# Phase 3 of a convolution and spectral-mix kernel on two 64-row tiles of the array

## The chip, the cores and the metric

The kernel runs on one core of a Trainium2 chip. The metric is device time in microseconds of one execution, the median of several runs. The core has a tensor engine (TensorE, PE in the profile, its weight loads PEld), a vector engine (VectorE, DVE), a scalar engine (ScalarE, ACT), GpSimd (POOL), and SyncE (SP), which here issues the transfers to DRAM.

## The reference

The input x has 8 batches, 3264 positions and 192 channels. First comes a causal convolution over 7 positions whose weights are a softmax per head (8 heads of 24 channels). Its result, called x from here on, goes through a spectral mix:

```
X = np.fft.rfft(x, axis=1)                        # the first 64 modes are kept
Yr = einsum('bmd,mde->bme', Xr, w_r) - einsum('bmd,mde->bme', Xi, w_i)
Yi = einsum('bmd,mde->bme', Xr, w_i) + einsum('bmd,mde->bme', Xi, w_r)
y = np.fft.irfft(Y, n=S, axis=1)
u = x + y
return u + np.maximum(u @ w_ch, 0.0)
```

The output is float32, 8 x 3264 x 192.

## The kernel before

A batch's 3264 positions are cut into 27 windows of 122 positions; a window is held as 128 rows, of which the last 6 belong to the next window too. `x_all` holds all of it in bf16, positions on the partitions.

Phase 1 loads x (GpSimd issues the transfers, which also change the type), convolves on TensorE with banded matrices, and sums the Fourier transform of the 64 modes. Phase 2 mixes the modes, four at a time on four column tiles of the array (`mix`, L387 to L402), and beside each group of modes it transposes pieces of `x_all` on TensorE (`t_next`, L354 to L370). The transposes go to `cTs[p]`, one for each pair p of batches: for each window first 128 channels of one batch, then 128 channels of the other, and then, in a slot for both, the remaining 64 channels of the one in rows 0 to 63 and of the other in rows 64 to 127 (its source is copied together by `make_tail`, L317). In the version before, pair p holds batches b and b + 2 with b from `pair_batch`.

Phase 3 computes the output. A group is half the batches, h, and a window w: four batches, two banks of PSUM, one bank for k = 0 and one for k = 1, each with two batches of 192 columns. The steps of one group are

- `group_g(..., 0, ...)` (L455): for each bank one product of the inverse transform's matrix `gst` (64 modes, real and imaginary parts, so 128 rows) with `zw`, the mixed modes already multiplied by w_ch; 384 columns. This is y @ w_ch.
- `group_ab` (L436): x @ w_ch, for each batch a product over 128 channels (L446) and one over the remaining 64 (L452), 192 columns each. For the second, the stationary operand has 128 rows, 64 of each batch of the pair; the moving operand `wB0` or `win1` holds w_ch's last 64 rows against the batch's own and zeros against the others.
- `relu` (L460) on ScalarE, in place in PSUM, both banks at once.
- `finish_group` (L467): `group_g` with part 1 adds y itself to the bank (384 columns again), VectorE adds x and writes the tile `t` (L470), and SP sends `t` to DRAM (L484), one transfer for a group, or two where a window must not write over the next one's rows.

The order is written out by hand (`tc.manual_schedule()`); each engine works through its own queue in that order, and semaphores are put in where data pass between engines. `seq` (L486 to L491) runs nine steps over three chains of windows, 0 to 8, 9 to 17 and 18 to 26, alternating the two halves h. A window's transfer writes 128 rows; the last 6 are not its own and are overwritten by the next window of the same batches, so the next window's transfer waits until this one has landed. SP's queue is in order, so whatever stands behind waits as well.

Groups are finished two behind the one whose products start. The first two groups get their x @ w_ch part before the last group of modes is mixed (L501 to L503, with a zeroing product over 384 columns, L439, since their first product then isn't the spectral one). Their spectral part follows the first half of the `zw` products (L524 to L528), and their ends follow the second half. Four PSUM tiles of two banks each (pools `pza`, `pzb`) go round; `t` has eight buffers (pool `p3`).

Of the kernel before, what the change touches and what calls it, by code (L numbers as in the profile page):

```python
# [9 lines left out]
ALU = mybir.AluOpType  # L10
ACT = mybir.ActivationFunctionType
AX = mybir.AxisListType
F32 = mybir.dt.float32
BF16 = mybir.dt.bfloat16
PSUM = bass.MemoryType.PSUM
# [3 lines left out]
def kernel(  # L19
# [9 lines left out]
    nc = tc.nc  # L29
    B, S, D = x.shape  # L30
# [5 lines left out]
    P = 128  # L36
    WIN = 122
    OV = KK - 1
    NWIN = 27
# [14 lines left out]
    x_all = constp.tile([P, B, NWIN, D], BF16, tag="x_all")  # L54
# [30 lines left out]
    xt = ep.tile([P, 4, 2 * B, MODES], BF16, tag="xt")  # L85
# [39 lines left out]
    for b in range(2, B):  # L125
        for u in range(3):
# [8 lines left out]
                            in0=sidx[:, :].unsqueeze(2).to_broadcast([P, NWIN, MODES]),  # L135
                            in1=midx[:, :].unsqueeze(1).to_broadcast([P, NWIN, MODES]),
                            op=ALU.mult)
# [8 lines left out]
                            in1=wmax[:, :].unsqueeze(2).to_broadcast([P, H, KK]), op=ALU.subtract)  # L146
# [24 lines left out]
    for k in range(KK):  # L171
        nc.vector.copy_predicated(
            out=cband[:, 0:4, :],
            mask=maskk[:, k, :].bitcast(mybir.dt.uint16).unsqueeze(1).to_broadcast([P, 4, P]),
            data=wpv[:, 0:4, k:k + 1].to_broadcast([P, 4, P]))
        for j in range(4):
# [3 lines left out]
                         start=(k == 0), stop=(k == KK - 1))  # L180
# [17 lines left out]
    win0 = constp.tile([P, 2 * D], BF16, tag="win0")  # L198
    win1 = constp.tile([P, 2 * D], BF16, tag="win1")
    wB0 = constp.tile([P, D], BF16, tag="wB0")  # L200
# [11 lines left out]
    gst = constp.tile([P, GW], BF16, tag="gst")  # L212
# [93 lines left out]
    conv_stack.close()  # L306
    workp = early_stack.enter_context(tc.tile_pool(name="work", bufs=2, side="right"))
    tailp = early_stack.enter_context(tc.tile_pool(name="tails", bufs=3, side="right"))
    pza = ctx.enter_context(tc.tile_pool(name="pza", bufs=2, space=PSUM))
    ps2 = ExitStack()  # L310
    pt = ps2.enter_context(tc.tile_pool(name="pt", bufs=4, space=PSUM))

    def pair_batch(p):
        return 4 * (p // 2) + p % 2

    tails = {}

    def make_tail(p, w0, n):  # L320
        b = pair_batch(p)
        tl = tailp.tile([P, 7, 2, D - P], BF16, tag="tail", name="tail")
        nc.vector.tensor_copy(out=tl[0:WIN, 0:n, :, :],
                              in_=x_all[0:WIN, b:b + 3:2, w0:w0 + n, P:D].rearrange("p b w e -> p w b e"))
        for w in range(w0, w0 + n):
            tails[(p, w)] = tl[0:WIN, w - w0, :, :].rearrange("p b e -> p (b e)")

    def slot_lhsT(p, k):
        b = pair_batch(p)
        r, w = divmod(k, NWIN)  # L330
        if r < 2:
            return x_all[0:WIN, b + 2 * r, w, 0:P]
        return tails[(p, w)]

    cTs = {}

    chunks = []
    for p in range(4):
        k = 0
        for i in range(11):  # L340
            n = 8 if i < 4 else 7
# [49 lines left out]
    def mix(g):  # L391
        zt = pt.tile([P, 512], F32, tag="p", name="yp")
        for j in range(3):
            for pos in range(4):
                m = MG * g + pos
                nc.tensor.matmul(zt[32 * pos:32 * pos + 32, 0:D],  # L396
                                 xt[:, j:j + 2, :, m].rearrange("p j k -> p (j k)"), wtiles[g][:, pos, j, :],
                                 start=(j == 0), stop=(j == 2), tile_position=(0, 32 * pos))
        ymix = workp.tile([P, D], BF16, tag="ymix")
        nc.scalar.copy(out=ymix[:], in_=zt[:, 0:D])  # L400
        return zt, ymix
# [7 lines left out]

    zwi = {}
    wBs = (wB0[:, :], win1[:, 0:D])

    def zw_mm(o, h, part, k):
        for i in range(2):
            b = 4 * h + 2 * k + i
            for e, wn in ((0, win0), (1, win1)):
                nc.tensor.matmul(o[:, D * i:D * i + D],
                                 yeT[:, e, :, :].rearrange("p m (c b) -> p (m c) b", c=2)[:, :, b],  # L420
                                 wn[:, D * part:D * part + D], start=(e == 0), stop=(e == 1),
                                 skip_group_check=True)
# [10 lines left out]
                nc.scalar.activation(out=zt[:], in_=zp[:, 0:2 * D], func=ACT.Copy, scale=ascale[:, 0:1])  # L433
            zwi[(h, part, k)] = zt[:]

    def group_ab(h, w, zp, first):  # L436
        if first:
            for k in range(2):
                nc.tensor.matmul(zp[:, k, 0:2 * D], xt[:, 3, 0:2, :].rearrange("p a m -> p (a m)"),  # L439
                                 win0[:, :], start=True, stop=False,  # L440
                                 skip_group_check=True)
        for k in range(2):
            for i in range(2):
                p, r = 2 * h + i, k
                c0 = WIN * (NWIN * r + w)
                nc.tensor.matmul(zp[:, k, D * i:D * i + D], cTs[p][:, c0:c0 + P], win0[:, 0:D],  # L446
                                 start=False, stop=False, skip_group_check=True)
        for i in range(2):
            for k in range(2):
                p = 2 * h + i  # L450
                c0 = WIN * (2 * NWIN + w)
                nc.tensor.matmul(zp[:, k, D * i:D * i + D], cTs[p][:, c0:c0 + P], wBs[k],  # L452
                                 start=False, stop=(i == 1 and not first), skip_group_check=True)

    def group_g(h, w, zp, part, first, last):  # L455
        for k in range(2):
            nc.tensor.matmul(zp[:, k, 0:2 * D], gst[:, WIN * w:WIN * w + P], zwi[(h, part, k)],  # L457
                             start=first, stop=last, skip_group_check=True)

    def relu(zp):  # L460
        nc.scalar.activation(out=zp[:, :, 0:2 * D], in_=zp[:, :, 0:2 * D], func=ACT.Relu)  # L461

    CH = 9

    def finish_group(h, w, zp):  # L467
        group_g(h, w, zp, 1, False, True)
        t = p3.tile([P, B // 2, D], F32, tag="t", name="t")
        nc.vector.tensor_tensor(  # L470
            out=t[:].rearrange("p (k i) e -> p k i e", k=2),
            in0=zp[:, :, 0:2 * D].rearrange("p k (i e) -> p k i e", i=2),
            in1=x_all[:, 4 * h:4 * h + 4, w, :].rearrange("p (k i) e -> p k i e", k=2),
            op=ALU.add)
        if w == NWIN - 1:
            rows = ((0, 80), (80, LASTVALID))
        elif w % CH == CH - 1:
            rows = ((0, 112), (112, WIN))
        else:
            rows = ((0, P),)  # L480
        for r0, r1 in rows:
            dst = bass.AP(tensor=out.tensor, offset=out.offset + (4 * h * S + WIN * w + r0) * D,
                          ap=[[D, r1 - r0], [S * D, B // 2], [1, D]])
            nc.sync.dma_start(out=dst, in_=t[r0:r1, :, :])  # L484

    steps = [(0, 0), (0, 1)]  # L486
    for st in range(CH):
        steps.append((1, st))
        if st + 2 < CH:
            steps.append((0, st + 2))  # L490
    seq = [(h, st + CH * c) for h, st in steps for c in range(3)]  # L491

    ahead(0)
    gq = [0, 1]
    zps = []
    for g in range(NGRP):
        last = g == NGRP - 1
        if last:
            while tpos[0] < len(chunks):
                t_next(3)  # L500
            zps = [pza.tile([P, 2, 512], F32, tag="z", name="z") for _ in range(2)]  # L501
            for n in range(2):
                group_ab(*seq[n], zps[n], True)  # L503
        m = mix(g)
        if g == 6:
            wts0_stack.close()
            cTb = ctx.enter_context(tc.tile_pool(name="stashb", bufs=1)).tile([P, CTW], BF16, tag="cTb")
            nc.vector.memset(cTb[:, NSLOT * WIN:CTW], 0.0)
            cTs[3] = cTb[:, :]
        if g in (0, 1, 2):  # L510
            load_weights(g + 7, wp)
        elif 7 <= g and g + 3 < NGRP:
            load_weights(g + 3, wp)
        if not last:
            for _ in range(1 if g < 7 else 2):
                t_next(2 if g < 6 else 3)
            if gq and g % 2 == 1:
                g_part(gq.pop(0))
        mix_t(g, *m)
    early_stack.close()  # L520
    p3 = ctx.enter_context(tc.tile_pool(name="p3", bufs=8, side="right"))
# [1 line left out]

    zw_part(0, 0)  # L524
    zw_part(0, 1)
    for n in range(2):
        group_g(*seq[n], zps[n], 0, False, False)
        relu(zps[n])  # L528
    zw_part(1, 0)
    zw_part(1, 1)  # L530
    for n in range(2):
        finish_group(*seq[n], zps[n])
    ps2.close()
    pzb = ctx.enter_context(tc.tile_pool(name="pzb", bufs=2, space=PSUM))

    zq = []
    for n in range(2, len(seq)):
        h, w = seq[n]
        zp = (pzb, pza)[n // 2 % 2 == 0].tile([P, 2, 512], F32, tag="z", name="z")
        group_g(h, w, zp, 0, True, False)  # L540
        group_ab(h, w, zp, False)
        relu(zp)
        zq.append((h, w, zp))
        while len(zq) > (2 if n < len(seq) - 6 else 1):
            finish_group(*zq.pop(0))
    while zq:
        finish_group(*zq.pop(0))

# [1 line left out]
_INS = ['x', 'weight', 'moe_w_r', 'moe_w_i', 'moe_w_ch']  # L550
# [26 lines left out]
```

## Time and profile before

| what | us |
|---|---|
| median of 3 runs | 196.57 (196.34 to 198.24) |
| the profiled execution, its own time | 196.34 |
| its span, first to last instruction | 194.6 |
| TensorE products, busy | 160.4 |
| VectorE, busy | 118.3 |
| ScalarE, busy | 112.0 |
| GpSimd, busy | 53.6 |
| first output transfer issued | 119.05 |
| last add of VectorE ends | 189.03 |
| last large output transfer issued | 189.74 |

Times in the profile are counted from the span's start. A line of a group gives the line of the kernel, the engine, the operation, what it writes and reads, how often, then its busy time and the mean duration of one in ns, then the idle time of the engine just before them and what ended it. Durations of products include their passage through the array, so products that follow each other overlap, and their rhythm is read from where they start. In the table by stages the columns are named in its first line; "DMA share" is the sum of the packets' times over 16 transfer engines. A stretch of the timeline gives start, length, engine, line and the number of instructions merged.

### The profile page before, as it was taken

The numbers are of one execution on the slowest core, as the hardware profiler recorded it, in microseconds if no ns is written. First come the engines' busy times: TensorE is split into PE (matmuls) and PEld (weight loads), VectorE is DVE, ScalarE is ACT, GpSimd is POOL, SyncE is SP. The second block draws the span as 40 slices with busy tenths as digits, with TensorE's granted clock in tenths as the row PEclk, the third lists the DMA queues.
The fourth block names the chain that finished last, engine by engine and source line by source line (L and its number), as shares of the span: only waits on it lengthen the run. The fifth ranks groups of instructions, "written<-read, shape, count | busy, mean of one in ns | idle before, by whom it ended". The sixth has DMA issues, their size and how long they took to land. (4 is left out here: it accounts for less than half of the span.)

```text
span 194.6 us, 4291 instructions
## 1 busy us (share of the span) xinstructions
PE 160.4 (82%) x1722; PEld 128.3 (66%) x1722; DVE 118.3 (61%) x185; ACT 112.0 (58%) x163; POOL 53.6 (28%) x89
## 2 busy tenths in 40 slices
PE   0147559988987987989889889999999999999950
PEld 0003338876976875878768767788788778878730
DVE  7896424543434443576785736677777777777860
ACT  2495692456656542768676546556655655665530
POOL 7999544332522943502452000000000000000000
PEclk9999999999999996999999999999999999999995
DMA  2999999999999999999999702699999999999995
GB/s 20 150 156 192 192 192 192 192 192 193 193 193 192 196 202 206 207 207 196 197 198 202 122 0 80 214 300 295 310 302 291 314 301 284 314 308 295 266 304 147
DMA packets 65443, 41.38 MB, mean 213 GB/s; under 512 B 29968, under 2 KB 65424, under 8 KB 65424
## 3 DMA queue, kind: packets, MB, share of 16 engines
q0 software_dynamic: 37088, 20.14, 75.8%
q1 hardware_dynamic: 28336, 20.97, 35.6%
q8 instruction: 13, 0.21, 0.5%
q14 instruction: 6, 0.05, 0.1%
HBM read 40.31 MB, written 20.94 MB: 315 GB/s over the span
## 5 line engine op out<-in xcount | busy, mean ns | idle before, releaser
L470 DVE TENSOR_TENSOR t<-z,x_all 128x768 f32<-128x768 f32 x54 | 51.4, 957 | 19.6 <-PE z L457 19.2
L461 ACT ACTIVATE z<-z 128x768 f32<-128x768 f32 x54 | 42.8, 795 | 27.5 <-PE z L452 26.1
L457 PE MATMUL z<-zw,gst 128*128 128x384 bf16 x216 | 44.4, 326 | 1.1 <-ACT z L461 0.6
L242 ACT CAST x_all<-cp 122x768 bf16<-122x768 f32 (+2 forms) x32 | 26.9, 878 | 23.4 <-PE cp L235 22.6
L235 PE MATMUL cp<-x_all,cband 128*128 128x240 bf16 (+2 forms) x192 | 27.5, 286 | 8.0 <-DVE x_all L230 3.2
L244 DVE CAST x_all<-cp 122x960 bf16<-122x960 f32 (+2 forms) x16 | 17.0, 1064 | 22.5 <-PE cp L235 22.4
L235 PEld LDWEIGHTS <-cband 128*128 128x128 bf16 x192 | 19.4, 108 | 14.9 <-issue 7.0
L61 POOL DMA_DIRECT2D x_all<-in_x_dram x24 | 23.9, 1003 | 15.2 <-DMA x_all<-in_x_dram 15.2
L457 PEld LDWEIGHTS <-gst 128*128 128x128 bf16 x216 | 20.3, 98 | 8.6 <-issue 1.7
L446 PE MATMUL z<-win,cTa 128*128 128x192 bf16 x162 | 24.4, 246 | 0.0
L255 PE MATMUL xp<-x_all,fst 122*128 122x192 bf16 (+1 forms) x216 | 22.9, 255 | 0.9 <-DVE x_all L244 0.5
L255 PEld LDWEIGHTS <-fst 122*128 122x128 bf16 (+1 forms) x216 | 18.9, 102 | 2.2 <-DVE x_all L244 0.7
L369 ACT COPY cTa<-tp 128x854 bf16<-128x854 bf16 (+1 forms) x16 | 14.5, 910 | 8.1 <-PE tp L363 8.0
L446 PEld LDWEIGHTS <-cTa 128*128 128x128 bf16 x162 | 15.0, 98 | 5.3
L452 PE MATMUL z<-wB,cTa 128*128 128x192 bf16 x81 | 17.7, 246 | 0.0
L452 PE MATMUL z<-win,cTa 128*128 128x192 bf16 x81 | 17.7, 246 | 0.0
L223 POOL DMA_DIRECT2D wt<-in_moe_w_r_dram x16 | 9.9, 619 | 25.5 <-PE yp L396 20.4
L367 DVE COPY cTa<-tp 128x854 bf16<-128x854 bf16 (+1 forms) x17 | 10.6, 626 | 8.5 <-PE tp L363 8.3
L363 PE MATMUL tp<-ident,x_all 122*128 122x122 bf16 x216 | 15.0, 224 | 0.0
L179 PE MATMUL bps<-scaled,ident 128*128 128x512 bf16 x7 | 4.1, 585 | 12.5 <-ACT scaled L177 12.5
L452 PEld LDWEIGHTS <-cTa 128*128 128x128 bf16 x162 | 14.2, 98 | 0.0
L363 PEld LDWEIGHTS <-x_all 122*128 122x128 bf16 x216 | 12.6, 101 | 1.6 <-issue 0.6
(87 smaller groups left out, 180.1 us busy)
## 6 DMA issues: line engine op xcount, KB each, us to landing
out_dram<-t SPq DMA_DIRECT2D x48, 384.0 KB, 3.5
wt<-in_moe_w_r_dram POOLq DMA_DIRECT2D x16, 288.0 KB, 6.2
wt<-in_moe_w_i_dram POOLq DMA_DIRECT2D x16, 288.0 KB, 7.0
x_all<-in_x_dram POOLq DMA_DIRECT2D x8, 432.0 KB, 14.4
x_all<-in_x_dram POOLq DMA_DIRECT2D x9, 384.0 KB, 17.8
x_all<-in_x_dram POOLq DMA_DIRECT2D x7, 480.0 KB, 17.7
out_dram<-t SPq DMA_DIRECT2D x4, 336.0 KB, 3.2
out_dram<-t SPq DMA_DIRECT2D x2, 240.0 KB
```

Of the source, the lines that this page charges most:

```text
L61: nc.gpsimd.dma_start(out=x_all[:, b, c0:c0 + n, :], in_=src)
L235: nc.tensor.matmul(cp[:, j, 0:GRP * n].rearrange("p (w e) -> p w e", w=n), cband[:, h, :], x_all[:, b, w0:w0 + n, GRP * h:GRP * h + GRP], ...
L242: nc.scalar.copy(out=dst, in_=srcv)
L244: nc.vector.tensor_copy(out=dst, in_=srcv)
L255: nc.tensor.matmul(xp[:, 0:D], fst[0:k, c, :], x_all[0:k, b, c, :], start=(c == 0), stop=(c == NWIN - 1))
L363: nc.tensor.transpose(tp[:, WIN * k:WIN * k + WIN], slot_lhsT(p, k0 + k), ident[0:WIN, 0:WIN])
L369: nc.scalar.copy(out=dst, in_=tp[:, 0:WIN * n])
L446: nc.tensor.matmul(zp[:, k, D * i:D * i + D], cTs[p][:, c0:c0 + P], win0[:, 0:D], start=False, stop=False, skip_group_check=True)
L452: nc.tensor.matmul(zp[:, k, D * i:D * i + D], cTs[p][:, c0:c0 + P], wBs[k], start=False, stop=(i == 1 and not first), skip_group_check=True)
L457: nc.tensor.matmul(zp[:, k, 0:2 * D], gst[:, WIN * w:WIN * w + P], zwi[(h, part, k)], start=first, stop=last, skip_group_check=True)
L461: nc.scalar.activation(out=zp[:, :, 0:2 * D], in_=zp[:, :, 0:2 * D], func=ACT.Relu)
L470: nc.vector.tensor_tensor(out=t[:].rearrange("p (k i) e -> p k i e", k=2), in0=zp[:, :, 0:2 * D].rearrange("p k (i e) -> p k i e", i=2), i ...
```

## The change

All of phase 3's products run on two row tiles of the array, rows 0 to 63 and rows 64 to 127. The group becomes a unit of two batches and one bank (h, w, k), and the pairs of the transposes become batches 2p and 2p + 1, so that a unit needs one `cTs` only. A unit's products are split into those of the upper rows (r = 0) and those of the lower rows (r = 1): for each r the spectral product, one product over 64 channels for each of the two batches, and one over the remaining 64 channels of batch r; this last one now has 64 rows and no zeros. Both halves add into the same bank, so they are not to run at the same time: the upper rows of unit j are issued in turn with the lower rows of unit j − 2. That the upper rows are done is told through GpSimd: an instruction of GpSimd that does nothing waits for the last upper product, and the first lower product waits for GpSimd. The product that adds y is split the same way, the upper rows of unit j − 4 beside the lower rows of unit j − 5.

ScalarE's relu and VectorE's add work on one unit, 384 columns; a `t` is still filled by two units and sent once. The order of windows is new: chains 0 to 7, 8 to 15 and 16 to 26, merged by a key, the first six windows of half 0 ahead. The first four units get their x @ w_ch part on the whole array early, and all `zw` products come before the first spectral product.

```diff
-    pza = ctx.enter_context(tc.tile_pool(name="pza", bufs=2, space=PSUM))
+    pza = ctx.enter_context(tc.tile_pool(name="pza", bufs=4, space=PSUM))
...
-        b = pair_batch(p)
+        b = 2 * p
...
+    def ab_full(u, zp):
+        h, w, k = u
+        nc.tensor.matmul(zp[:, 0:2 * D], xt[:, 3, 0:2, :].rearrange("p a m -> p (a m)"), win0[:, :],
+                         start=True, stop=False, skip_group_check=True)
+        for i in range(2):
+            for c0, wv in ((WIN * (NWIN * i + w), win0[:, 0:D]),
+                           (WIN * (2 * NWIN + w), (wB0[:, :], win1[:, 0:D])[i])):
+                nc.tensor.matmul(zp[:, D * i:D * i + D], cTs[2 * h + k][:, c0:c0 + P], wv,
+                                 start=False, stop=False, skip_group_check=True)
...
+    def z_ops(u, zp, r, filled):
+        h, w, k = u
+        lo, hi = 64 * r, 64 * r + 64
+        cTp = cTs[2 * h + k]
...
+            return nc.tensor.matmul(o, lhsT, rhs, start=start, stop=stop, skip_group_check=True,
+                                    tile_position=(lo, 0))
+
+        ops = [lambda: mm(zp[:, 0:2 * D], gst[lo:hi, WIN * w:WIN * w + P], zwi[(h, 0, k)][lo:hi, :],
+                          r == 0 and not filled, False)]
+        if not filled:
             for i in range(2):
+                c0 = WIN * (NWIN * i + w)
+                ops.append(lambda i=i, c0=c0: mm(zp[:, D * i:D * i + D], cTp[lo:hi, c0:c0 + P],
+                                                 win0[lo:hi, 0:D], False, False))
+            c0 = WIN * (2 * NWIN + w)
+            ops.append(lambda: mm(zp[:, D * r:D * r + D], cTp[lo:hi, c0:c0 + P],
+                                  (wB0[0:64, :], win1[64:P, 0:D])[r], False, False))
+        return ops
...
+    def run_pair(ops0, ops1, behind):
...
+        word = None
+        for i in range(max(len(ops0), len(ops1))):
+            if i < len(ops0):
+                ins = ops0[i]()
+                if i == len(ops0) - 1:
+                    word = nc.gpsimd.nop()
+                    tc.add_manual_dep(word.ins, ins.ins.name, SYNC, reason="row tile 0 is done")
+            if i < len(ops1):
+                ins = ops1[i]()
+                if i == 0:
+                    tc.add_manual_dep(ins.ins, behind.ins.name, SYNC, reason="row tiles on one bank")
+        return word
...
+    CHAINS = ((0, 8), (8, 16), (16, 27))
+    ENDS = (7, 15)
+    order = sorted((i / (12 if c == 2 else 10), c, w) for c, (a, e) in enumerate(CHAINS)
+                   for i, w in enumerate(range(a, e)))
+    order = [w for _, _, w in order]
+    LEAD = 6
+    wq = [(0, w) for w in order[0:LEAD]]
+    for i in range(NWIN):
+        wq.append((1, order[i]))
+        if i + LEAD < NWIN:
+            wq.append((0, order[i + LEAD]))
+    seq = [(h, w, k) for h, w in wq for k in range(2)]
...
+    for j in range(N + 6):
+        o0, o1 = [], []
+        if j < N:
+            if j >= 4:
+                zps.append((pza if j % 8 < 4 else pzb).tile([P, 512], F32, tag="z", name="z"))
+            o0 = z_ops(seq[j], zps[j], 0, j < 4)
+        if 0 <= j - 2 < N:
+            o1 = z_ops(seq[j - 2], zps[j - 2], 1, j - 2 < 4)
+        zword[j] = run_pair(o0, o1, zword.get(j - 2))
+        if 0 <= j - 2 < N:
+            relu(zps[j - 2])
+        o0, o1 = [], []
+        if 0 <= j - 4 < N:
+            o0 = y_ops(seq[j - 4], zps[j - 4], 0)
+        if 0 <= j - 5 < N:
+            o1 = y_ops(seq[j - 5], zps[j - 5], 1)
+        yword[j - 4] = run_pair(o0, o1, yword.get(j - 5))
+        if 0 <= j - 5 < N:
+            finish_unit(seq[j - 5], zps[j - 5])
```

`y_ops` gives for r the product of `gst` with part 1 of `zw`, on the rows of r; `finish_unit` is `finish_group` for one unit, with the transfer after k = 1. In the built program the waits for GpSimd's words stand on the weight loads of the lower y products; those of the lower z products are covered by them, since GpSimd's words come in order.

More of the change, by code (lines that the diff above doesn't have):

```diff
@@ L308 @@
     tailp = early_stack.enter_context(tc.tile_pool(name="tails", bufs=3, side="right"))
-    pza = ctx.enter_context(tc.tile_pool(name="pza", bufs=2, space=PSUM))
+    pza = ctx.enter_context(tc.tile_pool(name="pza", bufs=4, space=PSUM))
     ps2 = ExitStack()
     pt = ps2.enter_context(tc.tile_pool(name="pt", bufs=4, space=PSUM))
-    def pair_batch(p):
-        return 4 * (p // 2) + p % 2
     tails = {}
     def make_tail(p, w0, n):
-        b = pair_batch(p)
+        b = 2 * p
         tl = tailp.tile([P, 7, 2, D - P], BF16, tag="tail", name="tail")
         nc.vector.tensor_copy(out=tl[0:WIN, 0:n, :, :],
-                              in_=x_all[0:WIN, b:b + 3:2, w0:w0 + n, P:D].rearrange("p b w e -> p w b e"))
+                              in_=x_all[0:WIN, b:b + 2, w0:w0 + n, P:D].rearrange("p b w e -> p w b e"))
         for w in range(w0, w0 + n):
@@ L328, in slot_lhsT @@
     def slot_lhsT(p, k):
-        b = pair_batch(p)
         r, w = divmod(k, NWIN)
         if r < 2:
-            return x_all[0:WIN, b + 2 * r, w, 0:P]
+            return x_all[0:WIN, 2 * p + r, w, 0:P]
         return tails[(p, w)]
@@ L412 @@
     zwi = {}
-    wBs = (wB0[:, :], win1[:, 0:D])
     def zw_mm(o, h, part, k):
@@ L434, in zw_part @@
             zwi[(h, part, k)] = zt[:]
[L436 to L442, printed above, removed]
-            for i in range(2):
[L444 to L458, printed above, removed]
-    def relu(zp):
[L461 to L474, printed above, removed]
+    def ab_full(u, zp):
[7 more added lines that the diff above has]
+                                 start=False, stop=False, skip_group_check=True)
@@ new lines, in z_ops, with mm @@
+    def z_ops(u, zp, r, filled):
+        h, w, k = u
+        lo, hi = 64 * r, 64 * r + 64
+        cTp = cTs[2 * h + k]
+        def mm(o, lhsT, rhs, start, stop):
+            return nc.tensor.matmul(o, lhsT, rhs, start=start, stop=stop, skip_group_check=True,
[3 more added lines that the diff above has]
+        if not filled:
+            for i in range(2):
+                c0 = WIN * (NWIN * i + w)
[5 more added lines that the diff above has]
+        return ops
@@ new lines, in y_ops @@
+    def y_ops(u, zp, r):
+        h, w, k = u
+        lo, hi = 64 * r, 64 * r + 64
+        return [lambda: nc.tensor.matmul(zp[:, 0:2 * D], gst[lo:hi, WIN * w:WIN * w + P],
+                                         zwi[(h, 1, k)][lo:hi, :], start=False, stop=(r == 1),
+                                         skip_group_check=True, tile_position=(lo, 0))]
+    def relu(zp):
+        return nc.scalar.activation(out=zp[:, 0:2 * D], in_=zp[:, 0:2 * D], func=ACT.Relu)
+    SYNC = mybir.DependencyInfo(mybir.DependencyClass.Sync, mybir.DependencyReason.DATA)
@@ L475, in finish_group, with finish_unit @@
+    ts = {}
+    def finish_unit(u, zp):
+        h, w, k = u
+        if k == 0:
+            ts[h] = p3.tile([P, B // 2, D], F32, tag="t", name="t")
+        t = ts[h]
+        add = nc.vector.tensor_tensor(
+            out=t[:, 2 * k:2 * k + 2, :],
+            in0=zp[:, 0:2 * D].rearrange("p (i e) -> p i e", i=2),
+            in1=x_all[:, 4 * h + 2 * k:4 * h + 2 * k + 2, w, :], op=ALU.add)
+        if k == 0:
+            return
         if w == NWIN - 1:
             rows = ((0, 80), (80, LASTVALID))
-        elif w % CH == CH - 1:
+        elif w in ENDS:
@@ L484, in finish_group @@
             nc.sync.dma_start(out=dst, in_=t[r0:r1, :, :])
[L486 to L491, printed above, removed]
+    CHAINS = ((0, 8), (8, 16), (16, 27))
[10 more added lines that the diff above has]
+    seq = [(h, w, k) for h, w in wq for k in range(2)]
     ahead(0)
@@ L500 @@
                 t_next(3)
-            zps = [pza.tile([P, 2, 512], F32, tag="z", name="z") for _ in range(2)]
-            for n in range(2):
-                group_ab(*seq[n], zps[n], True)
+            zps = [pza.tile([P, 512], F32, tag="z", name="z") for _ in range(4)]
+            for n in range(4):
+                ab_full(seq[n], zps[n])
         m = mix(g)
@@ L525 @@
     zw_part(0, 1)
-    for n in range(2):
-        group_g(*seq[n], zps[n], 0, False, False)
-        relu(zps[n])
     zw_part(1, 0)
     zw_part(1, 1)
-    for n in range(2):
-        finish_group(*seq[n], zps[n])
     ps2.close()
[L534 to L547, printed above, removed]
+    pzb = ctx.enter_context(tc.tile_pool(name="pzb", bufs=4, space=PSUM))
+    N = len(seq)
+    zword, yword = {}, {}
+    for j in range(N + 6):
[17 more added lines that the diff above has]
+            finish_unit(seq[j - 5], zps[j - 5])
 _INS = ['x', 'weight', 'moe_w_r', 'moe_w_i', 'moe_w_ch']
```

## The prediction

> **What bounds the kernel now.** I read the table by stages first, then the chain in order of time, then the groups with their forms kept apart, and last the lines of the output transfer.
>
> ```profile
> core 0: us, PE busy (x) PEld busy (x) DVE busy (x) ACT busy (x) POOL busy (x), PEclk, DMA share, GB/s
> 119.00:130.00 11.00, 10.82 (x103) 8.78 (x102) 6.58 (x8) 6.37 (x9) 0.00 (x0) 1.00 0.73 225
> 130.00:185.00 55.00, 55.00 (x505) 44.08 (x504) 40.67 (x44) 33.38 (x42) 0.00 (x0) 1.00 0.98 298
> 185.00:188.00 3.00, 2.42 (x20) 1.47 (x17) 2.28 (x3) 1.59 (x2) 0.00 (x0) 1.00 1.06 333
> ```
>
> From 130 to 185 us TensorE never rests, at full granted clock, VectorE works 40.7 of 55 us, ScalarE 33.4, and GpSimd does nothing. But the output moves 298 GB/s with the transfer engines' share at 0.98: a second resource near its end. In the last stretch, with work queued, it moved 333 GB/s.
>
> ```profile
> 129.95 0.65 PE z L457 x4
> 130.60 0.33 PE z L446 x4
> 130.93 0.33 PE z L452 x4
> 131.26 0.65 PE z L457 x4
> ```
>
> One window of four batches takes 131.26 − 129.95 = 1.31 us of TensorE, all of it products: four of 384 columns at 0.65/4 = 0.162 us and eight of 192 at 0.082 us. So phase 3 is TensorE's.
>
> ```profile
> L470 DVE TENSOR_TENSOR t<-z,x_all 128x768 f32<-128x768 f32 x54 | 51.4, 957 | 19.6 <-PE z L457 19.2 <-issue 0.3
> L461 ACT ACTIVATE z<-z 128x768 f32<-128x768 f32 x54 | 42.8, 795 | 27.5 <-PE z L452 26.1 <-issue 1.3
> L269 DVE CAST xt<-tp 128x384 bf16<-128x384 f32 x8 | 4.4, 552 | 3.2 <-PE tp L267 3.2
> L433 ACT ACTIVATE zw<-zwps,ascale 128x384 bf16<-128x384 f32 x4 | 2.2, 584 | 1.7 <-PE zwps L419 1.7
> ```
>
> VectorE and ScalarE wait for TensorE; the last two rows give what half a window (384 columns from PSUM) costs them.
>
> ```profile
> 87.45 0.53 PE L396 MATMUL yp<-wt,xt 128*32 128x192 bf16 x12
> 87.92 1.03 PE L363 MATMUL tp<-ident,x_all 122*128 122x122 bf16 x16
> 91.38 0.54 PE L396 MATMUL yp<-wt,xt 128*32 128x192 bf16 x12
> 92.22 0.61 POOL L223 DMA_DIRECT2D wt<-in_moe_w_r_dram  x1 [1.19 <-PE yp L396]
> ...
> DMA to landing us min/median/max: 2.7/3.4/4.2
> ```
>
> The mix runs on four column tiles: twelve products of 192 columns in 0.53 us, where one after another they would need 12 × 0.082 = 0.98. Products on parts of the array do run together here. The transposes show that a 128-column weight load hides in (1.03 − 0.22)/15 = 0.054 us (0.22 is one transpose's own duration). GpSimd started 92.22 − (91.38 + 0.54) = 0.30 us after the product it waited for. The last line is for the output transfers at L484.
>
> **The change part by part.** A unit is half a window (two batches, one bank).
>
> *Columns.* Before, a unit streams 384 + 2 × 192 + 2 × 192 + 384 = 1536 columns, 1.31/2 = 0.655 us; the 2 × 192 at L452 carry 64 useful rows against 64 rows of zeros. After, each row tile streams 384 + 3 × 192 + 384 = 1344 columns per unit, beside the other tile's: 0.162 + 3 × 0.082 + 0.162 = 0.57 us, a window 1.14 us. The new pairing of batches (2p, 2p + 1) changes which data the same copies and transposes move, not their number. The first four units still get their part on the whole array, as the first two groups did.
>
> *Instructions.* A unit has 10 products and 10 loads instead of 6 and 6: 20 in 0.57 us, 28 ns each. The transposes sustain 32 in 0.86 us, 27 ns each. Nearly at that pace, so I add nothing but note it. Loads: if two tiles' loads went in turn, 10 × 0.054 = 0.54 us, still under 0.57; if each cost its listed 98 ns unhidden, 0.98 us. I take hidden, as whole-array loads are today. The Trainium skill (TensorE: Matmul & The Clock Gate, "The mechanism") says that a load overlaps running products only where its row group differs; taken literally five loads of a tile would stand bare, 5 × 0.054 more a unit, a window 1.68, and by the sum's formula below 219 us. The 83 ns rhythm of whole-array pairs here denies that reading.
>
> *GpSimd's words.* 216 waits that answer TensorE, in a queue that is empty here. An upper half's word is needed one iteration later by the weight load of the lower y product; behind that load stand the next unit's eight products, and behind these VectorE and ScalarE. Call the round trip s. Lower bound: in the timeline at 186.6 and 188.0 ScalarE and VectorE start 0.03 and 0.08 us after the product that releases them, so about 0.1 for both ways; upper: 0.30 to wake GpSimd, 0.04 for its wait, 0.05 back, 0.39. Iteration j's y start is at least 0.08 + 0.40 after the word of j−1, which is 0.326 + s after the y start of j−2: two iterations, that is one window, take at least 0.806 + s, between 0.91 and 1.20. I take it as hidden.
>
> *Evacuation.* VectorE: 957 − 384 × 1.04 = 557 ns, 1.04 from the two CAST forms at L244, (1158 − 958)/192; the 552 above agrees. 108 × 0.557 = 60.2 us against 51.4, 0.557 inside 0.57. ScalarE: about 0.48 to 0.58, also inside. Cover of 0.01 us is thin, but where two adds stood back to back (118.06, 1.82 us for two) they took 0.91 each, less than 0.957. The skill (TensorEngine Tiling (Array Packing), "PSUM Bottleneck") warns that tiling does not speed up what empties PSUM; by that, with a 0.045 us gap to each add, VectorE would set 0.60 a unit, and by the formula below the time would be 193.9.
>
> *Output.* 384 KB (393,216 bytes) per window at 333 GB/s is 1.18 us; at 298, 1.32; at a perfect pace, TensorE's 1.14. I take W = 1.16, between TensorE's and the queued rate, with 1.14 and 1.32 as ends.
>
> *Order of windows.* Every transfer writes 6 rows that the next window overwrites, so SP holds window w+1 until w landed, 3.4 us, and all transfers behind it. Before, successors are three groups apart or more. After, windows 16 and 17 follow each other at the start: SP stalls 3.4 − 1.16 = 2.2 us; eight t buffers hide it from VectorE, but if the transfers are at their limit it is lost: 0 to 2.2, I take 1.1. And 25 and 26 are adjacent at the very end: before, the last large transfer is issued 0.7 us after the last add (189.03 to 189.74); after, at 3.4 + 0.1 − 1.16 = 2.3. Costs 1.6 us.
>
> *Start and end of the loop.* After, all 32 zw products come first. TensorE is through at about 117.0 (114.06 + 2 × 1.5); then two units must go through g, word, lower g, relu 0.48, y, word, y, add: first window out at about 120.8. Before, the sixth window is out at 127.41, and at 1.31 backward that is 120.86 for the first: no difference. At the end, before gains 1.26 us on its own rhythm (189.03 against 127.41 + 48 × 1.31 = 190.29); after, the last unit saves some 0.6 of its iterations. Costs 0.66.
>
> **Sum.** Against the profiled execution, 196.34 us (span 194.6 and 1.7 around it; the median of the runs is 196.57): time = 196.34 + 1.6 + 0.66 + 1.1 − 53 × (1.31 − W). With W = 1.16: 199.7 − 7.95 = 191.75, about 191.8. Ends: W = 1.14 without the stall's 1.1, 189.6; W = 1.18 with 2.2, 193.9. Even with before is W = 1.25.
>
> **The rivals.**
> 1. *Output becomes the bound at today's rate.* W = 1.31, gain nil, and the later ends remain: 196.34 + 2.3 = 198.6. For it: share 0.98, and the rate is that of TensorE's rhythm almost to the byte. Against: 333 GB/s for 3 us when work was queued.
> 2. *GpSimd's round trip decides: slower.* W = 0.806 + s, from s = 0.44 on slower than before; at s = 0.6, W = 1.41 and 205. For it: its only row shows 0.30 just to wake. Against: that row includes starting a transfer, and nothing else is in its queue.
> 3. *The tiles do not run together.* W = 2 × 1.14 = 2.28: 251 us. The trace has column tiles only, no row tiles, and this product pair shares all output partitions. That is the case in which the change does not do what it says.
> 4. *They overlap with friction* (loads, issue pace, VectorE's thin cover): W = 1.22 to 1.30, 194.9 to 199.
>
> **How the numbers follow.** Forecast as summed 0.57; output 0.10; GpSimd 0.06; no concurrency 0.10; friction 0.17. A measurement of this kernel can tell about 1% from no change: 194.6 to 198.5 counts as same. Faster: 0.57 and 0.05 of friction, 0.62. Same: 0.10 of friction and 0.05 of output, 0.15. Slower: the rest, 0.23. The range goes from 189.0 (below W = 1.14 there is only measuring error) to 199.5, which takes in output and friction and leaves out about 0.16 above. The forecast's own range is 189.6 to 193.9.
>
> **What would show it.** Right: steady windows at 1.14 to 1.18 us in VectorE's rhythm; upper and lower products of a step starting a few ns apart, the next step 0.08 us later; output at 330 GB/s or more; SP idle about 2 us after the third output transfer and again before the last. Wrong: steps at twice 0.08 (rival 3); the y loads waiting for GpSimd (2); TensorE waiting for VectorE for want of a bank, or VectorE for t buffers that have not landed (1 or evacuation).

## The result, and the profile after

The changed kernel takes 202.49 us (median of 4 runs, 201.71 to 203.18) against 196.45 for the kernel before on the same chip: ratio 1.033, 95% interval 1.026 to 1.039. It is slower, where 191.8 was forecast. The profiled execution took 202.34 us, its span 200.5. Medians and ranges here and below take in every execution, while the ratios leave out those more than 1.5% above the fastest of their kernel.

The table by stages of the changed kernel, with the columns of the one shown for before:

```profile
core 0: us, PE busy (x) PEld busy (x) DVE busy (x) ACT busy (x) POOL busy (x), PEclk, DMA share, GB/s
122.00:140.00 18.00, 18.00 (x320) 16.94 (x317) 17.55 (x33) 14.98 (x32) 0.00 (x0) 1.00 0.83 255
140.00:187.00 47.00, 40.92 (x674) 32.66 (x668) 37.53 (x71) 32.49 (x69) 0.00 (x0) 1.00 0.97 295
187.00:200.50 13.50, 0.00 (x0) 0.00 (x0) 0.65 (x2) 0.00 (x0) 0.00 (x0) 0.52 0.66 185
```

Until 140 us TensorE never rests, and 320 products in 18 us are ten in 0.56 us. From then on it has holes, and the last 13.5 us hold hardly anything but transfers, at 185 GB/s. The chain in order of time shows the turn:

```profile
138.73 0.56 DVE t L501
139.29 0.01 issue
139.30 0.28 DVE t L501
139.59 5.10 DMA out_dram<-t
...
144.81 0.89 DVE t L501 x2
145.69 0.05 issue
145.75 1.04 DVE t L501 x2
146.79 0.01 issue
146.79 0.29 DVE t L501
147.09 6.11 DMA out_dram<-t
```

Before, TensorE's products were the chain from 119 to 187 us. Here it is VectorE's adds back to back up to 139.6 and then an output transfer, a few adds, another transfer. Who waited for whom on SP (us in sum, times, longest), in the kernel after from 118 us on and then in the kernel before from 125 us on:

```profile
SPq L516 <- DVE t L501: 37.9, 38, 8.6
SPq L516 <- DMA out_dram<-t: 19.2, 8, 3.8
```

```profile
SPq L484 <- DVE t L470: 37.8, 46, 1.2
SPq L484 <- DMA out_dram<-t: 2.0, 2, 1.3
```

SP waited 19.2 us for transfers to land, 2.0 before. From issue to landing a large transfer now takes longer, by the issue part of the page (median in us at the end), after and then before:

```profile
out_dram<-t SPq DMA_DIRECT2D x48, 384.0 KB, 5.0
```

```profile
out_dram<-t SPq DMA_DIRECT2D x48, 384.0 KB, 3.5
```

The transfers in the order of issue, from the trace, give six gaps of over 1 us between the end of one issue on SP and the start of the next. Distance is how many windows ahead the window stands whose rows this one overwrites:

| window sent (half, window) | issued at, us | gap before, us | distance |
|---|---|---|---|
| 0, 17 | 126.24 | 3.16 | 1 |
| 1, 17 | 139.12 | 3.82 | 2 |
| 0, 23 | 166.14 | 2.65 | 2 |
| 1, 23 | 180.97 | 1.74 | 2 |
| 0, 26 | 186.56 | 3.89 | 2 |
| 1, 26 | 196.72 | 3.42 | 1 |

They are all the transfers with a distance of 1 or 2; at distances of 3 to 8 no gap is over 0.75 us. They add up to 18.7 us. Each ends when the window before has landed, 3.46, 6.19, 4.97, 4.23, 5.06 and 3.91 us after its issue, in the order of the table.

The row tiles themselves did what they should. A stretch of the timeline (start, length, line), six products from 132.36 us on:

```profile
132.36 0.24 PE L449 MATMUL z<-win,cTb 64*128 64x192 bf16 x1
132.40 0.24 PE L449 MATMUL z<-win,cTa 64*128 64x192 bf16 x1
132.44 0.24 PE L449 MATMUL z<-win,cTb 64*128 64x192 bf16 x1
132.48 0.32 PE L467 MATMUL z<-zw,gst 64*128 64x384 bf16 x1
132.53 0.24 PE L449 MATMUL z<-wB,cTb 64*128 64x192 bf16 x1
132.61 0.32 PE L467 MATMUL z<-zw,gst 64*128 64x384 bf16 x1
```

Upper and lower products of 192 columns start 0.04 us apart, where one alone would need 0.082: they run side by side. VectorE and ScalarE by the groups with their forms kept apart:

```profile
L501 DVE TENSOR_TENSOR t<-z,x_all 128x384 f32<-128x384 f32 x108 | 58.4, 556 | 11.9 <-DMA out_dram<-t 6.7 <-PE z L449 2.1 <-PE z L467 1.9
L472 ACT ACTIVATE z<-z 128x384 f32<-128x384 f32 x108 | 51.0, 475 | 15.4 <-PE z L449 5.7 <-ACT z L472 0.3
```

556 ns and 475 ns, and VectorE's longest wait in sum is for transfers, 6.7 us: the t buffers, filled and not yet sent. SP holds them back.

### The profile page after: what moved, and what is told of

It is laid out like the page before. It is cut to its first block, busy times and chain, and to the rows that moved or that the text cites. A ratio compares the mean times of both kernels' runs of the same rounds, so it can differ in the third digit from the quotient of the medians.

```text
span 200.5 us, 5507 instructions
## 1 busy us (share of the span) xinstructions
PE 154.5 (77%) x2146; PEld 127.0 (63%) x2146; DVE 125.2 (62%) x239; ACT 120.4 (60%) x217; POOL 53.6 (27%) x89
## 4 chain that ended last, share of the span: by engine, by line
PE 33%; DVE 30%; DMA 16%; ACT 10%; issue 3%; DVEq 0%; ACTq 0%
DVE t L501 17%; DMA out_dram<-t 16%; PE cp L235 9%; PE tp L359 9%; PE xp L255 7%; DVE x_all L244 4%; ACT scaled L177 4%; PE yp L392 3%; ACT x_all L242 3%; DVE tail L320 2%; DVE cTa L363 2%; PE zwps L415 1%; PE tp L267 1%; ACT fst L190 1%; PE z L449 1%
## 5 line engine op out<-in xcount | busy, mean ns | idle before, releaser
L501 DVE TENSOR_TENSOR t<-z,x_all 128x384 f32<-128x384 f32 x108 | 58.4, 556 | 11.9 <-DMA out_dram<-t 6.7
L472 ACT ACTIVATE z<-z 128x384 f32<-128x384 f32 x108 | 51.0, 475 | 15.4 <-PE z L449 5.7
L449 PE MATMUL z<-zw,gst 64*128 64x384 bf16 x216 | 41.9, 323 | 3.8 <-DVE t L501 3.8
L467 PE MATMUL z<-zw,gst 64*128 64x384 bf16 x216 | 42.5, 323 | 0.2
L449 PE MATMUL z<-win,cTa 64*128 64x192 bf16 x385 | 40.6, 243 | 0.0
L449 PEld LDWEIGHTS <-cTa 64*128 64x128 bf16 x462 | 32.2, 94 | 5.0
L449 PEld LDWEIGHTS <-gst 64*128 64x128 bf16 x216 | 16.5, 94 | 6.2 <-issue 5.7
L449 PE MATMUL z<-wB,cTa 64*128 64x192 bf16 x77 | 18.7, 243 | 0.0
L449 PE MATMUL z<-win,cTb 64*128 64x192 bf16 x135 | 18.3, 243 | 0.0
L363 DVE COPY cTa<-tp 128x854 bf16<-128x854 bf16 (+1 forms) x17 | 10.6, 625 | 8.6 <-PE tp L359 8.3
L467 PEld LDWEIGHTS <-gst 64*128 64x128 bf16 x216 | 14.5, 94 | 0.9 <-POOLq L484 0.9
L449 PEld LDWEIGHTS <-cTb 64*128 64x128 bf16 x162 | 13.5, 94 | 2.0
```

The source lines that it names most:

```text
L363: nc.vector.tensor_copy(out=dst, in_=tp[:, 0:WIN * n])
L449: return nc.tensor.matmul(o, lhsT, rhs, start=start, stop=stop, skip_group_check=True, tile_position=(lo, 0))
L467: return [lambda: nc.tensor.matmul(zp[:, 0:2 * D], gst[lo:hi, WIN * w:WIN * w + P], zwi[(h, 1, k)][lo:hi, :], start=False, stop=(r == 1), ...
L472: return nc.scalar.activation(out=zp[:, 0:2 * D], in_=zp[:, 0:2 * D], func=ACT.Relu)
L501: add = nc.vector.tensor_tensor(out=t[:, 2 * k:2 * k + 2, :], in0=zp[:, 0:2 * D].rearrange("p (i e) -> p i e", i=2), in1=x_all[:, 4 * h + ...
```

## The experiments

Theory: the loss comes from the new order of windows, which puts some windows one or two places behind the one whose rows they overwrite; SP waits until that one has landed (3.5 to 6.2 us after its issue, by the six cases above), with everything else behind it, and the transfers' queue runs dry. Rivals: the row tiles or GpSimd's words hurt after all; the transfers' rate alone is the bound; too few t buffers. Ratios are to the kernel before on the same chip.

**Old order on the row tiles.**

```diff
-    CHAINS = ((0, 8), (8, 16), (16, 27))
-    ENDS = (7, 15)
...
-    wq = [(0, w) for w in order[0:LEAD]]
...
+    CH = 9
+    ENDS = (8, 17)
+    steps = [(0, 0), (0, 1)]
+    for st in range(CH):
+        steps.append((1, st))
+        if st + 2 < CH:
+            steps.append((0, st + 2))
+    wq = [(h, st + CH * c) for h, st in steps for c in range(3)]
```

> Changed kernel, but with the windows in the order of the kernel before (three chains of nine, successors of one half six windows apart, only at the start and the end three). Theory (order): what the change lost is idle time of the output transfers, which SP makes when a window's successor stands right behind it and SP must wait 5 to 6 us until the first has landed. Then SP's waits for landings shrink from 19 us to under 5, the transfers run at their queued 320 GB/s (393,216 bytes, 1.22 us a window), and the time is 120.5 + 53 x 1.22 + 5.5 + 1.9 = 192.5, between 191.5 and 194. Rival (the 64-row tiles or GpSimd's words disturb something else in the loop): still 199 to 203. Rival (transfers cannot hold 320 GB/s for long): 195 to 198.

Measured: 193.71 us (192.36 to 194.72), ratio 0.982 (0.976 to 0.988). SP's waits, and the chain in steady state:

```profile
SPq L516 <- DVE t L501: 50.1, 47, 8.4
SPq L516 <- DMA out_dram<-t: 2.6, 3, 1.1
```

```profile
140.23 0.24 PE z L467 x2
140.48 0.33 PE z L449 x6
140.80 0.24 PE z L467 x2
141.05 0.33 PE z L449 x6
```

All but 2.6 us of the waits are gone, TensorE's rhythm is 141.05 − 140.48 = 0.57 us a unit, as forecast, and the change is a gain. What made it slow is the order.

**Halves strictly in turn.**

```diff
+    wq = [(h, st + CH * c) for st in range(CH) for h in range(2) for c in range(3)]
```

> Changed kernel with three chains of nine windows and the two halves strictly in turn, so that every window's successor is six windows (7 us) behind it, at the start and the end too. Theory (order): no wait of SP for a predecessor is left, 191 to 193, at most 1 us better than with the order of before. Rival (the loss is elsewhere): 199 to 203.

Measured: 193.15 us (191.78 to 196.18), ratio 0.977 (0.971 to 0.983). At the upper end of what was expected, and the profile has no wait of SP for a landing. The difference to the old order (0.982) lies inside the intervals.

**The new order on the whole array.** The kernel before with the order of the change.

```diff
-    seq = [(h, st + CH * c) for h, st in steps for c in range(3)]
+    CHAINS = ((0, 8), (8, 16), (16, 27))
...
+    seq = wq
```

> Kernel before, whole array, but with the windows in the order of the changed kernel (chains 0-7, 8-15, 16-26, first six windows of half 0 ahead). Theory (order): the same stalls at a slower rhythm, at the adjacent windows 16 and 17 some 2.1 us that buffers absorb in part, and at the adjacent 25 and 26 at the end 2 us or more that nothing absorbs: 198.5 to 202. Rival (order innocent): 195.5 to 197.5.

Measured: 201.92 us (200.87 to 202.56), ratio 1.024 (1.018 to 1.029). SP's waits:

```profile
SPq L483 <- DVE t L469: 28.4, 32, 7.7
SPq L483 <- DMA out_dram<-t: 17.3, 7, 3.4
```

At the upper end of the expectation. The order alone costs the kernel before 2.4%. On the row tiles it costs more: 1.033/0.982 = 1.052.

**No overlapping rows.**

```diff
         else:
-            rows = ((0, P),)
+            rows = ((0, 112), (112, WIN))
```

> Changed kernel in its own order, but every window is sent as rows 0 to 111 and rows 112 to 121, so that no transfer writes over another's rows and none has to wait for a predecessor; 4.7% fewer bytes, twice as many transfers. Theory (order): the stalls vanish although adjacent windows stay adjacent; at 320 GB/s 20.05 MB take 62.7 us, and the time is 188.5 to 192. Rival (many small transfers cost SP and the queues more than the waits did): 195 to 200. Rival (the loss is in the tiles): no better than 200.

Measured: 205.46 us (204.71 to 207.88), ratio 1.042 (1.034 to 1.050): a miss, and slower than the 195 to 200 of the rival with many small transfers. The rival in the tiles ("no better than 200") fits the number, but the run with the old order has the same tiles. The stage from 130 to 180 us:

```profile
130.00:180.00 50.00, 45.05 (x744) 37.07 (x740) 38.56 (x74) 35.25 (x75) 0.00 (x0) 1.00 0.92 254
```

SP waits for no landing here, but the output moves at 254 GB/s instead of 320. One large and one 10-row transfer after the other are slower than one of 128 rows. Why (the engines that 10 rows reach, or the issue on SP) was not separated. The waits for a predecessor are gone here, but the lower rate hides what that gains.

**Half the bytes, both orders, and the kernel before.** Only in the transfers:

```diff
-            rows = ((0, P),)
+            rows = ((0, 64),)
```

> Changed kernel in its own order, but only rows 0 to 63 of each window are sent (half the bytes, the other output rows are left out). Theory (the rate of the queued transfers, about 320 GB/s, makes a stall cost what it does): a transfer of 192 KB lands in some 2.7 us and the queue is drained at half the load, so SP catches up after each stall, TensorE keeps its 1.145 us a window to the end, and the time is 120.5 + 53 x 1.145 + 5 + 1.9 = 188, up to 190. If the stalls cost by themselves, without the rate: 195 or more.

> Alternating order, again only rows 0 to 63 of each window sent. It shows what the row tiles give when the output does not bound: 121 + 53 x 1.145 + 4 + 1.9 = 187.6, 186.5 to 189; against the 193.2 of all bytes the difference is what the transfer rate costs. Rival (VectorE or GpSimd sets the rhythm and not the transfers): within 1 us of 193.

> Kernel before, whole array, only rows 0 to 63 of each window sent (the other output rows are left out). Theory (TensorE bounds the kernel before and its transfers hide): the rhythm stays 1.31 us a window and only the last transfers land earlier, 194 to 196. Beside the 185.7 of the tiles with half the bytes this gives the row tiles' own worth, some 9 us, of which 3.5 are left when all bytes are sent in the old order. Rival (the transfers already slow the kernel before): under 192.

Measured: 188.34, 185.74 and 194.23 us (the last of 8 runs, 193.58 to 197.01). The stage from 130 to 170 us is the same in both orders; first the new order, then the alternating one:

```profile
130.00:170.00 40.00, 40.00 (x704) 37.58 (x701) 38.96 (x71) 33.17 (x71) 0.00 (x0) 1.00 0.89 175
```

```profile
130.00:170.00 40.00, 40.00 (x704) 37.55 (x700) 38.99 (x70) 33.17 (x71) 0.00 (x0) 1.00 0.89 175
```

With half the bytes in the new order TensorE does not stop in this stage. But the edit does more than halve the bytes: rows 0 to 63 of a window are not rows that another window writes, so no transfer has to wait for a predecessor. SP's waits in the new order, with none for a landing:

```profile
SPq L516 <- DVE t L501: 62.2, 53, 9.1
```

Window 17 of half 0 is issued at 125.29 us, and window 16 lands only at 126.94. So these runs do not test whether a queue with room makes up for a wait, as the first expectation has it. They show that the new order without its waits, at half the bytes, hardly slows the loop. The two orders end 188.34 − 185.74 = 2.6 us apart, but in the profiled executions 2.2 us of that lie before the first transfer (issued at 121.90 and at 119.70 us). Counted from there, the executions take 66.4 and 66.0 us. The order does not set this start: in the other three runs of the new order on row tiles it lies between 120.47 and 123.14. With all bytes the same count gives 81.9 us for the new order and 73.6 for the old one, a difference of 8.3, and by the ratios the order costs about 10 (0.052 of 193.7).

That a wait is dear because the transfers are at their limit is argued from rates and not shown by itself. At 320 GB/s a window of 393,216 bytes takes 1.23 us, and on the row tiles TensorE makes one every 1.14, so nothing can be made up. The kernel before makes one every 1.31 us, and there the same order, with 17.3 us of waits against 19.2, costs 2.4% and not 5.2%.

The kernel before gains only 2.4 us from half the bytes; the row tiles against it are worth 194.23 − 185.74 = 8.5 us when the output does not bound (the two orders differ, 3 and 6 windows at the ends), and 3.5 with all bytes. The alternating run came out 0.8 us below its range; its first transfer left at 119.70 us, where the sum had 121. The 4 us for the end were right (last transfer issued at 179.85, span 184.0).

**A slower word from GpSimd.**

```diff
+                    if slow:
+                        ms = nc.gpsimd.memset(pad[:], 0.0)
+                        word = nc.gpsimd.nop()
+                        tc.add_manual_dep(word.ins, ms.ins.name, SYNC, reason="slow word")
```

> Alternating order, with a GpSimd memset of 128 x 384 (0.44 us by its row in the profile before) put between the end of each upper y product and its word, so that the round trip s is some 0.65 us instead of 0.1 to 0.2. My bound was W = 0.806 + s a window: 1.45 us, so the end of VectorE's work moves from about 184 to 199 and the time to 203 to 207. If GpSimd's answer is hidden by more than the two iterations that I counted, under 197.

Measured: 204.91 us, ratio 1.043 (1.037 to 1.050). The chain of its steady state:

```profile
150.66 0.41 PE z L467 x2
...
152.13 0.41 PE z L467 x2
```

A window takes 152.13 − 150.66 = 1.47 us, 1.45 was worked out. The round trip can be read from the timeline (start, length): an upper y product, GpSimd's memset behind it, the weight load of the lower y product, and the next upper y product behind that:

```profile
150.43 0.32 PE L467 MATMUL z<-zw,gst 64*128 64x384 bf16 x1
...
150.94 0.42 POOL L489 MEMSET pad<- 128x384 bf16 x1 [0.32 <-PE z L467]
...
151.46 0.09 PEld L467 LDWEIGHTS <-gst 64*128 64x128 bf16 x1 [0.21 <-POOLq L490]
...
151.89 0.32 PE L467 MATMUL z<-zw,gst 64*128 64x384 bf16 x1
```

The product ends at 150.75, so s = 151.46 − 150.75 = 0.71 us, and 0.32 + 0.71 + 0.43 = 1.46. The bound has the right form; its constant of 0.806 was 0.05 too long. GpSimd could have made this change slow, but with the plain word it does not: in the changed kernel the weight loads of the lower y products waited for it 0.9 us in all.

**Two issuing engines.**

```diff
+            if h == 0:
+                nc.sync.dma_start(out=dst, in_=t[r0:r1, :, :])
+            else:
+                late.append((dst, t[r0:r1, :, :]))
...
+            nc.scalar.dma_start(out=dst, in_=src)
```

> Alternating order, but the transfers of half 1 are issued by ScalarE, two units late, and those of half 0 by SP. Theory A (320 GB/s is what the 16 engines give to 768-byte rows from one core): no faster rate, 192 to 195, or worse where a held-up issue delays a relu. Theory B (320 GB/s is the limit of one queue): over 340 GB/s and 189 to 191.

Measured: 194.97 us (192.40 to 195.38), ratio 0.986 (0.976 to 0.996).

```profile
130.00:170.00 40.00, 40.00 (x701) 36.16 (x698) 38.80 (x71) 32.11 (x70) 0.00 (x0) 1.00 1.04 319
```

And one queue, in the changed kernel between its stalls:

```profile
142.00:162.00 20.00, 18.64 (x321) 15.38 (x318) 16.38 (x31) 15.20 (x32) 0.00 (x0) 1.00 1.04 321
```

319 GB/s from two queues, 321 from one: theory B is out, and the time is that of theory A. What sets the 320 (the rows of 768 bytes, the engines or the memory) no run here shows. The Trainium skill (DMA: Bandwidth & Descriptors, "Issuing engines are not separate DMA queues") says that transfers run on the same 16 engines whoever issues them, and that several issuing engines save time in issuing only. This run agrees. SP itself waited 14.4 of these 40 us for landings, with the rate no lower: half of the transfers came from ScalarE.

**Ten buffers.**

```diff
-    p3 = early_stack.enter_context(tc.tile_pool(name="p3", bufs=8, side="right"))
+    p3 = early_stack.enter_context(tc.tile_pool(name="p3", bufs=10, side="right"))
```

> Changed kernel with 10 buffers for t instead of 8 (12 do not fit). Theory (SP and the rate of its transfers set the end; VectorE and TensorE wait only because the t buffers are full of what SP holds back): VectorE's waits for transfers shrink from 6.7 us to 2 to 5 and the time stays within 1 us of the changed kernel's 202.5. Rival (too few buffers are the cause): 200 or less.

Measured: 203.65 us (202.22 and 205.07), ratio 1.038 (1.030 to 1.046). The waits of the engines and of SP:

```profile
DVE t L501 <- DMA out_dram<-t: 3.6, 3, 1.9
...
SPq L516 <- DMA out_dram<-t: 17.2, 7, 3.8
```

VectorE waits half as long for buffers, SP nearly as long as before, and nothing is won (the time is 1.15 us above the 202.5, where less than 1 was expected; the ratios are 1.038 and 1.033). The buffers only pass the hold-up on.

**An earlier start.** `zw_part(1, 0)` and `zw_part(1, 1)` moved to the loop's iteration 4, alternating order.

> Alternating order, and the zw products of half 1 moved behind the spectral products of the first four units, so that the first output leaves up to 1 us earlier. As the transfers run at their 320 GB/s from the first to the last, the end should move by what the start moves: 192.0 to 193.2 against the alternating order's 193.2. If the start does not set it: 193 to 194.

Measured: 193.35 us (192.49 to 194.60), ratio 0.987 (0.982 to 0.991). No better than the alternating order. The first transfer leaves at 120.58 us; in the other runs of the alternating order on the row tiles it leaves between 119.70 and 123.93. So a move of up to 1 us can't be told in one trace, and the run says nothing about what an earlier start would give. Of the versions that send the whole output, those with the old and the alternating order beat both kernels, and so do the one with two issuing engines and this one.

## Why the prediction was wrong

- *Bound before, columns, instructions, GpSimd, evacuation: right.* Forecast 0.57 us a unit, measured 0.57; first window out at 120.8, measured 120.47 (so close partly by luck, since the start lies between 119.70 and 123.93 in the runs on row tiles); VectorE 557 ns, measured 556; word hidden, and the form of its bound confirmed by the slow word. On "PSUM Bottleneck" of the Trainium skill (TensorEngine Tiling (Array Packing)): VectorE does become the thinnest cover, 17.55 of 18 us busy, but the adds came 0.57 us apart, not the 0.60 that a gap at each would give.
- *Output: mis-sized.* I took W = 1.16 between TensorE's pace and a 333 GB/s row that lasted 3 us. With work queued it is 321 GB/s over 20 us in the changed kernel (the row from 142 us above) and 317 over 40 us with the old order:

```profile
130.00:170.00 40.00, 40.00 (x704) 37.57 (x700) 38.96 (x71) 33.19 (x70) 0.00 (x0) 1.00 1.03 317
```

At 320 a window takes 393,216/320 = 1.23 us. That is 53 × 0.07 = 3.7 us of the miss. A row of 3 us was too short to take a lasting rate from.
- *Order of windows: the step that failed.* It said "After, windows 16 and 17 follow each other at the start: SP stalls 3.4 − 1.16 = 2.2 us [...] I take 1.1. And 25 and 26 are adjacent at the very end [...] Costs 1.6 us." That is two gaps and 2.7 us. The trace has six gaps of 18.7 us in all, and the order cost about 10. Two errors. I looked for neighbours only, and missed the pairs at distance 2 (16/17 and 22/23 of half 1, 22/23 and 25/26 of half 0); by my own landing time of 3.4 us they would have stalled too, since two windows take only 2.3. And that 3.4 was measured with a light queue. It held about for the two pairs that I named (3.46 and 3.91 us), but at the four that I missed the landing took 4.2 to 6.2. The end of the loop shows the size: the last add ends at 187.65 us and the last large transfer is issued 9.1 us later, at 196.72, where I had 2.3 us. The rest of the 202.34 − 191.75 = 10.6 us, after the rate's 3.7, is this step: 6.9 us (a remainder, not measured by itself; the order's cost of 8 to 10 us, less the sum's 2.7, gives 5.6 to 7.3).
- *The cover went with it.* I let the eight buffers hide the stall at the start from VectorE. It waited 6.7 us for buffers in all. With a window made every 1.14 us and sent every 1.23, SP never catches up (argued from the rates, as said above).
- *Rivals.* The first one (output as the bound at today's rate, 198.6) was nearest in kind, but its price was for a rate of 298 GB/s, and the rate was better; what hurt was the queue running empty. None of the four named the order as a case of its own; it stood in the sum as a term with one value.
- With the order of before, the sum without its two order terms and with W = 1.23 gives 196.34 + 0.66 − 53 × 0.08 = 192.8; that run measured 193.7.

## What to carry to other kernels

When a change speeds up the engine that bounds, look at the resource next to it at once: here transfers at 298 GB/s had 7% left, and the change asked for 15. Where transfers must wait for an earlier one's landing in an in-order queue, list the distance of every such pair, not only of neighbours, and compare distance times rhythm with the landing time under the load that the change brings. When a change bundles a fast mechanism with a new order, run each alone: here one was worth −1.8% and the other +2.4%, together +3.3%.

## What the runs showed of the hardware

- Rows of 768 bytes leave this core at 317 to 321 GB/s when transfers are queued for 20 us or more, from one issuing engine or from two. While they are queued, SP's own time to issue one grows: median 372 ns before, 991 ns after, by the two lines below (minimum, median, maximum), kernel before first.

```profile
L484 SPq DMA_DIRECT2D out_dram<-t x60: 317/372/1479, 119.0 to 190.5; - x60
```

```profile
L516 SPq DMA_DIRECT2D out_dram<-t x60: 317/991/1611, 120.5 to 197.1; - x60
```

- The DMA share is no measure of how much room is left: with half the rows it read 0.89 at 175 GB/s, with all of them 0.98 at 298 and 1.04 at 319 and 321.
- Splitting a 122-row output into 112 and 10 rows lowered the rate to 254 GB/s.
- Two row tiles hold 0.04 us between alternating products of 192 columns, with a weight load before each, over tens of us, at full granted clock. The round trip of a word through GpSimd, 0.71 us with a 0.42 us memset in it, leaves about 0.29 us for the way there, the two waits and the way back.
